# Column loads turned into row loads plus TensorE transposes, and a third buffer for the attention weight groups, in a DMA-bound decode block with its backward pass

## The chip, the cores and the metric

The kernel runs on one core of one Trainium2 chip. The metric is the device time of one execution in microseconds (us), on the slowest core (here the only one). The trace is of one profiled execution, so its span is a little shorter than the timed number: 793.2 us of span belong to a time of about 795 us.

## The reference, cut to what matters

One token goes through an attention block with a cached K and V, and beside it through a SwiGLU MLP. The kernel computes the output and all gradients.

```python
# x: (1,1,640)  k_cache, v_cache: (1,32,8192,128)  wq: (640,4096)  wo: (4096,640)
# w1, w3: (640,1728)  w2: (1728,640); all bf16
xn  = layernorm(x)
q   = xn @ wq                                   # 32 heads of 128
p   = softmax(q . K^T * 128**-0.5)              # per head, 8192 keys
out = x + (p @ V) @ wo + (silu(xn @ w1) * (xn @ w3)) @ w2
# and by jax.vjp, for a given grad_out:
# dx, dk_cache, dv_cache, dwq, dwo, dw1, dw3, dw2
```

K and V of one head are 2 MB each, and so are dK and dV. Over 32 heads 134 MB come in and 134 MB go out; with the weights and their gradients the kernel moves 304.5 MB.

## The kernel before: the parts that matter here

SBUF holds nine 2 MB buffers for K and V tiles (`kv`). dK and dV are written in place into the buffers of K and V and stored from there, so a load of a later head waits for a store of an earlier one. Heads come in 8 groups of 4; each group has its slices of wq and wo (640 KB each), and dwq and dwo are again made in place. Big loads are issued on SyncE's queue (SP), in program order; stores on GpSimd's (POOL); the small loads of x and grad_out on ScalarE's (ACT).

```python
wpool = ctx.enter_context(tc.tile_pool(name="wp", bufs=2))          # L62
tpool = ctx.enter_context(tc.tile_pool(name="tp", bufs=3))          # L63
...
x_bc_bf = consts.tile([P, D], BF16, name="x_bc_bf")                 # L83
nc.scalar.dma_start(x_bc_bf[:], A_x.rearrange("a b d -> (a b d)").partition_broadcast(P))
g_bc = consts.tile([P, D], BF16, name="g_bc")
nc.scalar.dma_start(g_bc[:], grad_out.rearrange("a b d -> (a b d)").partition_broadcast(P))
x_col_bf = consts.tile([P, NC], BF16, name="x_col_bf")
g_col_bf = consts.tile([P, NC], BF16, name="g_col_bf")
with nc.allow_non_contiguous_dma(reason="tiny column-layout loads of x / grad_out"):
    nc.scalar.dma_start(x_col_bf[:], A_x.rearrange("a b (c p) -> p (a b c)", p=P))
    nc.scalar.dma_start(g_col_bf[:], grad_out.rearrange("a b (c p) -> p (a b c)", p=P))
...
def load_group(g):                                                  # L113
    wq_g = wpool.tile([P, NC, GW], BF16, name="wq_g", tag="wq_g")
    nc.sync.dma_start(wq_g[:], wq_v[:, :, g * GW:(g + 1) * GW])
    wo_g = wpool.tile([P, GH, D], BF16, name="wo_g", tag="wo_g")
    nc.sync.dma_start(wo_g[:], wo_v[:, g * GH:(g + 1) * GH, :])
...
nc.vector.tensor_copy(XN_rep[:], xn_col[:].unsqueeze(2).to_broadcast([P, NC, P]))   # L196
nc.vector.tensor_copy(G_rep[:], g_col[:].unsqueeze(2).to_broadcast([P, NC, P]))
...
def prep_group(g):                                                  # L212, start of a group
    for ci in range(NC):
        nc.tensor.matmul(ps_q[:, 0:GW], lhsT=XN_rep[:, ci, :], rhs=wq_g[:, ci, :],
                         start=(ci == 0), stop=(ci == NC - 1))
    ...
bc_sb = consts.tile([P, 2, F], BF16, name="bc_sb")                  # L394, kept to the end
...
for wi in range(2):                                                 # L453, in mlp()
    for b0 in range(0, NB, 4):
        dg = small.tile([P, 4, P // 2, 2], BF16, name="dgm", tag="dg", bufs=1)
        nc.vector.tensor_tensor(dg..., id2..., dgu2[:, wi, ...], ALU.mult)   # diagonal blocks
        nc.tensor.matmul(pb[:, 0:bn * P], lhsT=ones_bf[:], rhs=dg..., start=True, stop=True)
        nc.scalar.copy(bc_sb[:, wi, f0:f1], pb[:, 0:f1 - f0])                # a row on all partitions
...
for h in range(2, H):                                               # L519
    if hh == 1 and g + 1 < NG:
        load_group(g + 1)
    if hh == GH - 1 and g + 1 < NG:
        prep_group(g + 1)
    if h + 1 < H:
        phase_a(h + 1)     # scores, softmax, p @ V
        phase_t(h + 1)     # dP, dS
    phase_b(h)             # dV, dK in place, and their stores
    load_kv(2)
    if hh == GH - 1:
        finish_group(g)    # dwo, dwq in place, and their stores
...                        # dx, then:
mlp_grads()                # dW1 from bc_sb[:,0], dW3 from bc_sb[:,1], then dW2: 6.6 MB
```

The MLP itself runs early, between heads 2 and 3; its weights lie in four of the nine `kv` buffers until then. The gradients of its weights are made at the very end, in tiles oA (most of dW1), oB (most of dW3), oD (most of dW2) and oC (the rests of all three).

## Time and profile before

| What | Value |
|---|---|
| Time, median of 3 runs | 793.3 us (791.96 to 795.97) |
| Moved, mean over the span | 304.5 MB, 384 GB/s |
| Busy: DVE, PE, ACT | 69%, 74%, 40% |
| First projection matmul | 35.16 us |
| First and last dV store issued | 60.77 us and 755.70 us |

No compute engine is full and the DMA engines nearly are, so the question is where they are not. The table by windows gives, for each stretch, its length, the busy time of each engine (with its instructions in brackets), and at the end of each line the granted TensorE clock, the busy share of the DMA engines and the rate in GB/s. Kernel before:

```profile
core 0: us, PE busy (x) PEld busy (x) DVE busy (x) ACT busy (x) POOL busy (x), PEclk, DMA share, GB/s
0.00:51.50 51.50, 15.21 (x205) 11.46 (x205) 10.50 (x24) 13.88 (x17) 1.08 (x8) 1.00 0.97 364
51.50:62.00 10.50, 9.92 (x208) 9.56 (x207) 7.70 (x13) 6.99 (x10) 0.68 (x1) 0.84 0.03 8
62.00:150.00 88.00, 75.20 (x1244) 58.48 (x1242) 66.10 (x108) 32.48 (x49) 2.67 (x5) 0.77 0.89 347
150.00:720.00 570.00, 454.30 (x8407) 391.92 (x8404) 415.51 (x572) 253.32 (x351) 39.72 (x66) 0.78 1.00 410
720.00:750.00 30.00, 24.14 (x448) 20.16 (x447) 24.92 (x33) 8.53 (x14) 1.60 (x3) 0.77 0.51 212
750.00:793.20 43.20, 7.08 (x128) 5.93 (x127) 25.08 (x57) 3.16 (x5) 9.39 (x12) 0.50 0.92 354
235.00:520.00 285.00, 223.48 (x4123) 192.66 (x4121) 207.49 (x290) 120.80 (x170) 19.76 (x33) 0.78 1.00 406
```

Read the last two columns downwards. The middle is full. There are three holes: 51.5 to 62 (8 GB/s), 62 to 150 (347 GB/s) and 720 to 750 (212 GB/s). The reasons stand in the list of waits (engine and line that waited, what released it, then the total in us, how many times, the longest). Kernel before, lines picked out:

```profile
PE pF L217 <- DVE XN_rep L196: 35.2, 1, 35.2
PE pF L217 <- DMA wq_g<-in_A_wq_dram: 30.7, 4, 12.9
PE pT L234 <- DMA wo_g<-in_A_wo_dram: 22.9, 4, 7.6
...
DVE x_col L192 <- DMA x_col_bf<-in_A_x_dram: 16.4, 1, 16.4
DVE g_col L193 <- DMA g_col_bf<-in_grad_out_dram: 8.6, 1, 8.6
```

The same list for SyncE's own DMA queue, kernel before, one line:

```profile
SPq L115 <- DMA out_dram<-wq_g: 70.9, 6, 12.5
```

And the timeline of the kernel before (start, duration, engine, line, what it writes and reads; in square brackets the idle time before it and what ended it), a few lines of DVE, PE and POOL:

```profile
23.35 0.17 DVE L192 CAST x_col<-x_col_bf 128x5 f32<-128x5 bf16 x1 [16.38 <-DMA x_col_bf<-in_A_x_dram]
32.14 0.17 DVE L193 CAST g_col<-g_col_bf 128x5 f32<-128x5 bf16 x1 [8.62 <-DMA g_col_bf<-in_grad_out_dram]
...
653.56 1.04 PE L217 MATMUL pF<-wq_g,XN_rep 128*128 128x512 bf16 x2 [12.90 <-DMA wq_g<-in_A_wq_dram]
...
760.11 0.66 POOL L349 DMA_DIRECT2D out_dram<-Kt  x1 [3.87 <-DVE od_bf L355]
...
766.90 0.86 POOL L488 DMA_DIRECT2D out_dram<-oA  x1
769.19 0.75 POOL L491 DMA_DIRECT2D out_dram<-oB  x1 [1.43 <-DVE oB L490]
773.82 2.09 POOL L494 DMA_DIRECT2D out_dram<-oD  x1 [3.88 <-DVE oD L493]
```

Together they tell this. Two loads of 1.2 KB land at 23 and 32 us; the layernorm and with it all compute begins only then, at 35 us. By 51 us all nine buffers are full and nothing is finished, so nothing can be stored and nothing loaded: the first hole. At group starts TensorE waits for wq_g and wo_g (53.6 us in 8 waits), because their loads wait on the SP queue until the dwq store of two groups earlier has freed one of two buffers. The second hole (62 to 150 us) covers the MLP stage; these lines do not explain it, only that VectorE was busy 66 of its 88 us. The last stall at a group start ends at 653.56 us and leaves compute late for the last heads, where no loads are left to fill the queue: the last hole. In the tail the MLP gradients follow the last dK store closely (oA 6.8 us after it), because `bc_sb` has been ready since the MLP ran.

The queue that carried the x and grad_out loads, kernel before, from the page's table of DMA queues (packets, MB, share of the 16 engines' time):

```profile
q10 hardware_dynamic: 1600, 0.33, 0.3%
```

1600 packets for 0.33 MB: the column layout breaks into one packet of two bytes per element, 1280 of them for the two columns.

### The profile page before, as it was taken

How to read it: one execution, taken by the hardware profiler on the slowest of the kernel's cores; microseconds unless marked ns; L12 is line 12 of the kernel's file. 1: busy time of each engine (PE TensorE's matmuls, PEld its weight loads, DVE VectorE, ACT ScalarE, POOL GpSimd, SP SyncE). 2: the span in 40 equal slices, each digit the busy share in tenths (PEclk: the TensorE clock that was granted, in tenths of full speed). 3: DMA queues.
4: the chain of work that ended last, by engine and by line, in shares of the span. 5: the costliest groups of instructions: out<-in, count | busy, mean ns of one | idle time of the engine just before them, and what ended most of it. 6: DMA issues, size and time to landing. Idle time of an engine off the chain costs nothing. (4 is left out here: it accounts for less than half of the span.)

```text
span 793.2 us, 23350 instructions
## 1 busy us (share of the span) xinstructions
PE 585.9 (74%) x10623; PEld 497.5 (63%) x10623; DVE 549.8 (69%) x804; ACT 318.4 (40%) x444; POOL 55.1 (7%) x95
## 2 busy tenths in 40 slices
PE   0297889889885978699496968698696939699620
PEld 0175668788665966598376857597476827588520
DVE  1158469977758865888189845887289836788890
ACT  0072324554351843275153643285153634276010
POOL 0000000010000100010001000010001000010022
PEclk9996659968776976888587967789587967679555
DMA  8968988899999999999999999999999999996598
GB/s 323 379 247 326 383 339 321 335 411 419 416 430 373 426 417 419 379 409 409 428 406 389 426 416 425 362 422 419 428 410 389 425 421 408 380 420 285 242 390 303
DMA packets 36487, 304.51 MB, mean 384 GB/s; under 512 B 4148, under 2 KB 15348, under 8 KB 20004
## 3 DMA queue, kind: packets, MB, share of 16 engines
q1 hardware_dynamic: 21828, 151.35, 47.9%
q0 software_dynamic: 12960, 151.34, 46.1%
q8 instruction: 83, 1.36, 0.7%
q10 hardware_dynamic: 1600, 0.33, 0.3%
q14 instruction: 16, 0.13, 0.0%
HBM read 151.67 MB, written 151.34 MB: 382 GB/s over the span
## 5 line engine op out<-in xcount | busy, mean ns | idle before, releaser
L262 ACT COPY KT<-pT 128x1024 bf16<-128x1024 bf16 x256 | 242.6, 1038 | 48.5 <-PE pT L260 47.0
L305 PE MATMUL dp<-T,ident_bf 128*128 128x256 bf16 x1024 | 180.7, 312 | 1.7 <-issue 0.8
L260 PE MATMUL pT<-ident_bf,Kt 128*128 128x128 bf16 x2048 | 168.0, 228 | 0.0
L303 DVE TENSOR_TENSOR T<-Vt,do_g 128x2048 bf16<-128x2048 bf16 x128 | 154.3, 1215 | 11.4 <-ACT do_g L243 8.1
L260 PEld LDWEIGHTS <-Kt 128*128 128x128 bf16 x2048 | 131.2, 103 | 3.0 <-issue 0.5
L305 PEld LDWEIGHTS <-ident_bf 128*128 128x128 bf16 x1024 | 103.3, 111 | 25.3 <-issue 3.9
L265 PEld LDWEIGHTS <-KT 128*128 128x128 bf16 x2048 | 78.3, 98 | 35.8 <-ACT KT L262 24.7
L265 PE MATMUL sA<-qc_g,KT 128*128 128x1 bf16 x2048 | 89.0, 165 | 11.7 <-ACT KT L262 4.9
L323 PEld LDWEIGHTS <-Kt 128*128 128x128 bf16 x2048 | 59.3, 101 | 36.1 <-issue 34.8
L325 ACT COPY od_g<-sA 128x2 f32<-128x2 f32 x32 | 5.1, 160 | 164.8 <-PE sA L323 108.0
L287 PEld LDWEIGHTS <-Vt 128*128 128x128 bf16 x2048 | 56.4, 97 | 19.1 <-issue 17.3
L217 PE MATMUL pF<-wq_g,XN_rep 128*128 128x512 bf16 x40 | 18.6, 591 | 65.8 <-DVE XN_rep L196 35.2
L346 POOL DMA_DIRECT2D out_dram<-Vt x32 | 17.6, 549 | 519.4 <-DVE junk L314 244.2
L217 PEld LDWEIGHTS <-XN_rep 128*128 128x128 bf16 x40 | 3.7, 118 | 69.0 <-DVE XN_rep L196 35.2
L236 ACT COPY KT<-pT 128x1024 bf16<-128x1024 bf16 (+1 forms) x24 | 19.8, 874 | 54.7 <-PE pT L234 54.7
L318 DVE COPY negD<-sA 128x1 f32<-128x1 f32 x32 | 5.0, 155 | 47.3 <-PE sA L315 45.6
L271 DVE TENSOR_REDUCE gmax<-sA 1x1 f32<-1x128 f32 x32 | 8.8, 276 | 36.7 <-PE sA L269 36.6
L234 PE MATMUL pT<-ident_bf,wo_g 128*128 128x128 bf16 x160 | 17.2, 283 | 22.9 <-DMA wo_g<-in_A_wo_dram 22.9
L278 ACT ACTIVATE E<-sA,negM 128x64 f32<-128x64 f32 x32 | 10.4, 325 | 56.5 <-DVE negM L275 56.4
L234 PEld LDWEIGHTS <-wo_g 128*128 128x128 bf16 x160 | 14.6, 131 | 23.7 <-DMA wo_g<-in_A_wo_dram 23.5
L349 POOL DMA_DIRECT2D out_dram<-Kt x32 | 17.3, 542 | 151.5 <-DVE negM L275 40.2
L308 DVE TENSOR_REDUCE DP<-dp 128x64 f32<-128x256 f32 x32 | 13.3, 416 | 20.7 <-PE dp L305 20.7
(390 smaller groups left out, 841.1 us busy)
## 6 DMA issues: line engine op xcount, KB each, us to landing
Kt<-in_A_k_cache_dram SPq DMA_DIRECT2D x32, 2048.0 KB, 13.6
Vt<-in_A_v_cache_dram SPq DMA_DIRECT2D x32, 2048.0 KB, 12.0
out_dram<-Vt POOLq DMA_DIRECT2D x32, 2048.0 KB, 12.9
out_dram<-Kt POOLq DMA_DIRECT2D x32, 2048.0 KB, 14.2
wq_g<-in_A_wq_dram SPq DMA_DIRECT2D x8, 640.0 KB, 13.3
wo_g<-in_A_wo_dram SPq DMA_DIRECT2D x8, 640.0 KB, 23.2
out_dram<-wo_g POOLq DMA_DIRECT2D x8, 640.0 KB, 17.9
out_dram<-wq_g POOLq DMA_DIRECT2D x8, 640.0 KB, 18.9
```

Of the source, the lines that this page charges most:

```text
L217: nc.tensor.matmul(ps_q[:, 0:GW], lhsT=XN_rep[:, ci, :], rhs=wq_g[:, ci, :], start=(ci == 0), stop=(ci == NC - 1))
L234: nc.tensor.transpose(pT[:, k, :], wo_g[:, hh, ci * P:(ci + 1) * P], ident_bf[:])
L236: nc.scalar.copy(wT[:, 0:len(bl), :], pT[:, 0:len(bl), :])
L260: nc.tensor.transpose(pT[:, k, :], K3[:, 8 * c + k, :], ident_bf[:])
L262: nc.scalar.copy(KT[:], pT[:])
L265: nc.tensor.matmul(sA[:, j:j + 1], lhsT=KT[:, k, :], rhs=qcol, start=(j == 0), stop=True, skip_group_check=True)
L287: nc.tensor.matmul(sA[:, OC:OC + 1], lhsT=V3[:, j, :], rhs=P2[:, j, 0:1], start=False, stop=(j == J - 1), skip_group_check=True)
L303: nc.vector.tensor_tensor(T3, V3[:, :, ds_], do_h[:, ds_].unsqueeze(1).to_broadcast([P, J, QD]), ALU.mult)
L305: nc.tensor.matmul(dp[:], lhsT=ident_bf[:], rhs=T3[:, :, R * i:R * (i + 1)], start=(q == 0 and i == 0), stop=(q == DH // QD - 1 and i == Q ...
L323: nc.tensor.matmul(sA[:, OC + 1:OC + 2], lhsT=K3[:, j, :], rhs=U2[:, j, 0:1], start=False, stop=(j == J - 1), skip_group_check=True)
L346: nc.gpsimd.dma_start(dvc[h], Vt[:])
L349: nc.gpsimd.dma_start(dkc[h], Kt[:])
```

## The change

It has three parts. (1) x and grad_out come in as five rows of 256 bytes each, TensorE transposes them into columns, and the layernorm sums are made by a matmul with ones. The replicated tiles XN_rep and G_rep go; the matmuls read the column with stride 0 instead. (2) wq_g and wo_g get a third buffer each, so weights can come a group earlier. (3) These cost SBUF, and it is paid for by dropping `bc_sb` (6.9 KB per partition): the broadcast MLP rows are built one at a time in a T buffer (`make_bc`), once in the MLP and a second time for the gradients at the end.

```diff
-    x_bc_bf = consts.tile([P, D], BF16, name="x_bc_bf")
-    nc.scalar.dma_start(x_bc_bf[:], A_x.rearrange("a b d -> (a b d)").partition_broadcast(P))
+    xg_row = consts.tile([NC, 2, P], BF16, name="xg_row")
+    nc.scalar.dma_start(xg_row[:, 0, :], A_x.rearrange("a b (c p) -> (a b c) p", p=P))
+    nc.scalar.dma_start(xg_row[:, 1, :], grad_out.rearrange("a b (c p) -> (a b c) p", p=P))
 ...
-        nc.scalar.dma_start(x_col_bf[:], A_x.rearrange("a b (c p) -> p (a b c)", p=P))
-        nc.scalar.dma_start(g_col_bf[:], grad_out.rearrange("a b (c p) -> p (a b c)", p=P))
 ...
-        wq_g = wpool.tile([P, NC, GW], BF16, name="wq_g", tag="wq_g")
+        wq_g = wpool.tile([P, NC, GW], BF16, name="wq_g", tag="wq_g", bufs=3)
-        wo_g = wpool.tile([P, GH, D], BF16, name="wo_g", tag="wo_g")
+        wo_g = wpool.tile([P, GH, D], BF16, name="wo_g", tag="wo_g", bufs=3)
 ...
+    for i in range(2):
+        nc.tensor.transpose(ps_x[:, i, 0:NC], xg_row[:, i, :], ident_bf[0:NC, 0:NC])
+    nc.vector.tensor_copy(xg_col[:], ps_x[:, :, 0:NC])
 ...   # sums by matmul with ones_f instead of a reduction over x_bc_bf
-            nc.tensor.matmul(ps_q[:, 0:GW], lhsT=XN_rep[:, ci, :], rhs=wq_g[:, ci, :],
+            nc.tensor.matmul(ps_q[:, 0:GW], lhsT=xn_col_bf[:, ci:ci + 1].to_broadcast([P, P]), rhs=wq_g[:, ci, :],
 ...   # and the same for G_rep
-    bc_sb = consts.tile([P, 2, F], BF16, name="bc_sb")
+    def make_bc(wi):
+        bc = t_tile()
+        ...   # the loop over b0 from mlp(), still with one dg buffer, into bc
+        return bc
 ...
         for wi in range(2):                       # in mlp()
+            bc = make_bc(wi)
 ...
+        for wi in range(2):                       # in mlp_grads()
+            bc = make_bc(wi)
+            da, db, dv = ((d1a, d1b, dw1_v), (d3a, d3b, dw3_v))[wi]
+            ...   # dW1 or dW3 from bc, and their stores; dW2 follows as before
```

More of the change, by code (lines that the diff above doesn't have):

```diff
@@ L81 @@
     dw3_v = out_7.rearrange("(ci p) f -> p ci f", p=P)
-    x_bc_bf = consts.tile([P, D], BF16, name="x_bc_bf")
-    nc.scalar.dma_start(x_bc_bf[:], A_x.rearrange("a b d -> (a b d)").partition_broadcast(P))
+    xg_row = consts.tile([NC, 2, P], BF16, name="xg_row")
+    nc.scalar.dma_start(xg_row[:, 0, :], A_x.rearrange("a b (c p) -> (a b c) p", p=P))
+    nc.scalar.dma_start(xg_row[:, 1, :], grad_out.rearrange("a b (c p) -> (a b c) p", p=P))
     g_bc = consts.tile([P, D], BF16, name="g_bc")
     nc.scalar.dma_start(g_bc[:], grad_out.rearrange("a b d -> (a b d)").partition_broadcast(P))
-    x_col_bf = consts.tile([P, NC], BF16, name="x_col_bf")
-    g_col_bf = consts.tile([P, NC], BF16, name="g_col_bf")
-    with nc.allow_non_contiguous_dma(reason="tiny column-layout loads of x / grad_out"):
-        nc.scalar.dma_start(x_col_bf[:], A_x.rearrange("a b (c p) -> p (a b c)", p=P))
-        nc.scalar.dma_start(g_col_bf[:], grad_out.rearrange("a b (c p) -> p (a b c)", p=P))
     NB = (F + P - 1) // P
@@ L168 @@
     DXN0 = OUT0 + NC
-    negmean = consts.tile([P, 1], F32, name="negmean")
-    rstd = consts.tile([P, 1], F32, name="rstd")
-    x_col = consts.tile([P, NC], F32, name="x_col")
-    g_col = consts.tile([P, NC], F32, name="g_col")
-    xn_col = consts.tile([P, NC], F32, name="xn_col")
-    xn_col_bf = consts.tile([P, NC], BF16, name="xn_col_bf")
-    XN_rep = consts.tile([P, NC, P], BF16, name="XN_rep")
-    G_rep = consts.tile([P, NC, P], BF16, name="G_rep")
-    msum = small.tile([P, 1], F32, name="msum")
-    nc.vector.tensor_reduce(msum[:], x_bc_bf[:], AX.X, ALU.add)
-    nc.vector.tensor_scalar(negmean[:], msum[:], -1.0 / D, None, ALU.mult)
-    xc_t = tpool.tile([P, 1024], F32, name="xc", tag="T")
-    xc = xc_t[:, 0:D]
-    nc.vector.tensor_scalar(xc, x_bc_bf[:], negmean[:], None, ALU.add)
-    xsq_t = tpool.tile([P, 1024], F32, name="xsq", tag="T")
-    xsq = xsq_t[:, 0:D]
-    sumsq = small.tile([P, 1], F32, name="sumsq")
-    nc.vector.scalar_tensor_tensor(xsq, xc, 1.0, xc, ALU.mult, ALU.mult, accum_out=sumsq[:])
-    std = small.tile([P, 1], F32, name="std")
-    nc.scalar.activation(std[:], sumsq[:], ACTF.Sqrt, bias=eps_t[:], scale=1.0 / D)
-    nc.vector.reciprocal(rstd[:], std[:])
-    nc.vector.tensor_copy(x_col[:], x_col_bf[:])
-    nc.vector.tensor_copy(g_col[:], g_col_bf[:])
-    nc.vector.tensor_scalar(xn_col[:], x_col[:], negmean[:], rstd[:], ALU.add, ALU.mult)
-    nc.vector.tensor_copy(xn_col_bf[:], xn_col[:])
-    nc.vector.tensor_copy(XN_rep[:], xn_col[:].unsqueeze(2).to_broadcast([P, NC, P]))
-    nc.vector.tensor_copy(G_rep[:], g_col[:].unsqueeze(2).to_broadcast([P, NC, P]))
     def t_tile():
@@ L209, in pst_f @@
         return ps_t.tile([P, 512], F32, name="pF", tag="pT")
+    negmean = consts.tile([P, 1], F32, name="negmean")
+    rstd = consts.tile([P, 1], F32, name="rstd")
+    xg_col = consts.tile([P, 2, NC], F32, name="xg_col")
+    x_col = xg_col[:, 0, :]
+    g_col = xg_col[:, 1, :]
+    g_col_bf = consts.tile([P, NC], BF16, name="g_col_bf")
+    xn_col = consts.tile([P, NC], F32, name="xn_col")
+    xn_col_bf = consts.tile([P, NC], BF16, name="xn_col_bf")
+    ps_x = ps_t.tile([P, 2, 8], BF16, name="ps_x", tag="pT")
+    for i in range(2):
+        nc.tensor.transpose(ps_x[:, i, 0:NC], xg_row[:, i, :], ident_bf[0:NC, 0:NC])
+    nc.vector.tensor_copy(xg_col[:], ps_x[:, :, 0:NC])
+    nc.vector.tensor_copy(g_col_bf[:], g_col)
+    msum = small.tile([P, 1], F32, name="msum")
+    nc.vector.tensor_reduce(msum[:], x_col, AX.X, ALU.add)
+    ps_m = pst_f()
+    nc.tensor.matmul(ps_m[:, 0:1], lhsT=ones_f[:], rhs=msum[:], start=True, stop=True)
+    nc.vector.tensor_scalar(negmean[:], ps_m[:, 0:1], -1.0 / D, None, ALU.mult)
+    xc = small.tile([P, NC], F32, name="xc", bufs=1)
+    nc.vector.tensor_scalar(xc[:], x_col, negmean[:], None, ALU.add)
+    xsq = small.tile([P, NC], F32, name="xsq", bufs=1)
+    sumsq = small.tile([P, 1], F32, name="sumsq")
+    nc.vector.scalar_tensor_tensor(xsq[:], xc[:], 1.0, xc[:], ALU.mult, ALU.mult, accum_out=sumsq[:])
+    ps_v = pst_f()
+    nc.tensor.matmul(ps_v[:, 0:1], lhsT=ones_f[:], rhs=sumsq[:], start=True, stop=True)
+    std = small.tile([P, 1], F32, name="std")
+    nc.scalar.activation(std[:], ps_v[:, 0:1], ACTF.Sqrt, bias=eps_t[:], scale=1.0 / D)
+    nc.vector.reciprocal(rstd[:], std[:])
+    nc.vector.tensor_scalar(xn_col[:], x_col, negmean[:], rstd[:], ALU.add, ALU.mult)
+    nc.vector.tensor_copy(xn_col_bf[:], xn_col[:])
     def prep_group(g):
@@ L238, in prep_group @@
                 ci = bl[k0][0]
-                nc.tensor.matmul(ps_do[:, 0:GW], lhsT=G_rep[:, ci, :],
+                nc.tensor.matmul(ps_do[:, 0:GW], lhsT=g_col_bf[:, ci:ci + 1].to_broadcast([P, P]),
                                  rhs=wT[:, k0:k0 + GH, :].rearrange("p h d -> p (h d)"),
@@ L393 @@
     blocks_f = [(b, min(P, F - b * P)) for b in range(NB)]
-    bc_sb = consts.tile([P, 2, F], BF16, name="bc_sb")
+    dgu2 = consts.tile([P, 2, NB, 2], BF16, name="dgu2")
+    def make_bc(wi):
+        bc = t_tile()
+        id2 = ident_bf[:].rearrange("p (a b) -> p a b", b=2)
+        for b0 in range(0, NB, 4):
+            bn = min(4, NB - b0)
+            dg = small.tile([P, 4, P // 2, 2], BF16, name="dgm", tag="dg", bufs=1)
+            nc.vector.tensor_tensor(dg[:, 0:bn], id2.unsqueeze(1).to_broadcast([P, bn, P // 2, 2]),
+                                    dgu2[:, wi, b0:b0 + bn, :].unsqueeze(2).to_broadcast([P, bn, P // 2, 2]),
+                                    ALU.mult)
+            pb = pst_f()
+            nc.tensor.matmul(pb[:, 0:bn * P], lhsT=ones_bf[:],
+                             rhs=dg[:, 0:bn].rearrange("p k a b -> p (k a b)"), start=True, stop=True)
+            f0 = b0 * P
+            f1 = min(F, f0 + bn * P)
+            nc.scalar.copy(bc[:, f0:f1], pb[:, 0:f1 - f0])
+        return bc
     hcol = consts.tile([P, NB], F32, name="hcol")
@@ L449, in mlp @@
         nc.vector.tensor_tensor(dgu[:, 0, :], dgu[:, 0, :], t1[:], ALU.mult)
-        dgu2 = consts.tile([P, 2, NB, 2], BF16, name="dgu2")
         nc.vector.tensor_copy(dgu2[:], dgu[:].unsqueeze(3).to_broadcast([P, 2, NB, 2]))
-        id2 = ident_bf[:].rearrange("p (a b) -> p a b", b=2)
-        for wi in range(2):
-            for b0 in range(0, NB, 4):
-                bn = min(4, NB - b0)
-                dg = small.tile([P, 4, P // 2, 2], BF16, name="dgm", tag="dg", bufs=1)
-                nc.vector.tensor_tensor(dg[:, 0:bn], id2.unsqueeze(1).to_broadcast([P, bn, P // 2, 2]),
-                                        dgu2[:, wi, b0:b0 + bn, :].unsqueeze(2).to_broadcast([P, bn, P // 2, 2]),
-                                        ALU.mult)
-                pb = pst_f()
-                nc.tensor.matmul(pb[:, 0:bn * P], lhsT=ones_bf[:],
-                                 rhs=dg[:, 0:bn].rearrange("p k a b -> p (k a b)"), start=True, stop=True)
-                f0 = b0 * P
-                f1 = min(F, f0 + bn * P)
-                nc.scalar.copy(bc_sb[:, wi, f0:f1], pb[:, 0:f1 - f0])
         FC = 384
         for wi in range(2):
+            bc = make_bc(wi)
             wa, wb = ((w1a, w1b), (w3a, w3b))[wi]
@@ L473, in mlp @@
                 nc.vector.tensor_tensor(T3[:, 0:NA, :], wa[:, :, f0:f0 + fn],
-                                        bc_sb[:, wi, f0:f0 + fn].unsqueeze(1).to_broadcast([P, NA, fn]), ALU.mult)
-                nc.vector.tensor_tensor(T3[:, NA, :], wb[:, f0:f0 + fn], bc_sb[:, wi, f0:f0 + fn], ALU.mult)
+                                        bc[:, f0:f0 + fn].unsqueeze(1).to_broadcast([P, NA, fn]), ALU.mult)
+                nc.vector.tensor_tensor(T3[:, NA, :], wb[:, f0:f0 + fn], bc[:, f0:f0 + fn], ALU.mult)
                 for i in range(fn // RX):
@@ L485, in mlp_grads @@
         d1a, d3a, d1b, d3b, d2a, d2b = split_views(oA, oB, oC, oD)
-        for ci in range(NA):
-            nc.vector.tensor_scalar(d1a[:, ci, :], bc_sb[:, 0, :], xn_col[:, ci:ci + 1], None, ALU.mult)
-        nc.gpsimd.dma_start(dw1_v[:, 0:NA, :], d1a)
-        for ci in range(NA):
-            nc.vector.tensor_scalar(d3a[:, ci, :], bc_sb[:, 1, :], xn_col[:, ci:ci + 1], None, ALU.mult)
-        nc.gpsimd.dma_start(dw3_v[:, 0:NA, :], d3a)
+        for wi in range(2):
+            bc = make_bc(wi)
+            da, db, dv = ((d1a, d1b, dw1_v), (d3a, d3b, dw3_v))[wi]
+            for ci in range(NA):
+                nc.vector.tensor_scalar(da[:, ci, :], bc[:, 0:F], xn_col[:, ci:ci + 1], None, ALU.mult)
+            nc.gpsimd.dma_start(dv[:, 0:NA, :], da)
+            nc.vector.tensor_scalar(db, bc[:, 0:F], xn_col[:, NA:NC], None, ALU.mult)
+            nc.gpsimd.dma_start(dv[:, NA, :], db)
         for b in range(NBA):
@@ L494, in mlp_grads @@
         nc.gpsimd.dma_start(out_8[0:NBA * P, :].rearrange("(fb p) c -> p fb c", p=P), d2a)
-        nc.vector.tensor_scalar(d1b, bc_sb[:, 0, :], xn_col[:, NA:NC], None, ALU.mult)
-        nc.gpsimd.dma_start(dw1_v[:, NA, :], d1b)
-        nc.vector.tensor_scalar(d3b, bc_sb[:, 1, :], xn_col[:, NA:NC], None, ALU.mult)
-        nc.gpsimd.dma_start(dw3_v[:, NA, :], d3b)
         for b in range(NBA, NB):
@@ L539 @@
     nc.vector.tensor_tensor(dxn[:], acc_sb[:, NC:2 * NC], dxm[:], ALU.add)
-    nc.vector.tensor_tensor(fin[:, 0:NC], acc_sb[:, 0:NC], x_col[:], ALU.add)
+    nc.vector.tensor_tensor(fin[:, 0:NC], acc_sb[:, 0:NC], x_col, ALU.add)
     st = consts.tile([P, 2], F32, name="st")
@@ L551 @@
     nc.vector.tensor_scalar(t5[:], t5[:], nst[:, 0:1], rstd[:], ALU.add, ALU.mult)
-    nc.vector.tensor_tensor(fin[:, NC:2 * NC], t5[:], g_col[:], ALU.add)
+    nc.vector.tensor_tensor(fin[:, NC:2 * NC], t5[:], g_col, ALU.add)
     ps_o = pst_f()
```

## The prediction

> **What bounds the kernel now.** The table by windows gives the DMA engines' busy share: 1.00 from 150 to 720 us (410 GB/s), where only bytes count. Three holes are not DMA-bound: 51.5-62 us (share 0.03, about 10 us lost), 62-150 us (0.89, 10 us) and 720-750 us (0.51, 15 us). The queue table's shares sum to 95%: about 754 of 793 us are DMA work, 40 us gaps.
>
> Hole 1: in the timeline TensorE starts at 35.2 us. The waits blame x_col_bf (16.4 us, landed 23.3) and g_col_bf (8.6 more, landed 32.1). All nine K/V buffers are full by 51 us, but the first store is issued at 60.8, 25.6 us after compute began. The Trainium skill ("DMA: Bandwidth & Descriptors", Rules for kernel authors) says a strided last dimension lowers to one descriptor per element; the trace agrees: two 1.2 KB loads needed 21 and 30 us, and their queue moved 1600 packets for 0.33 MB.
>
> Hole 3: at group starts TensorE waits for wq_g (30.7 us in 4 waits, longest 12.9) and wo_g (22.9 us in 4), because the load waits on the SP queue for the dwq store of two groups earlier (70.9 us, 6 waits). The last stall, 640.5-653.6 us, leaves compute late for the last heads; the DMA runs dry at 720-750.
>
> **What the change does.**
> 1. Column loads become row loads of five 256-byte runs, then some 12 small dependent steps, estimated at 4-5 us from steps of 0.15-0.35 us in the trace. XN_rep and G_rep (0.8 us each) go. Compute should start near 9-11 us, limited by wq_g too (landing 7-9 us): 25 us earlier. The DMA can use only the gaps of 51-150 us: 16-20 us gained.
> 2. Third wq_g/wo_g buffer: weights arrive one group ahead, so TensorE's wait for them vanishes. The instruction order shows the SP queue still waiting for a dwq store in nearly the same place, now for a later group, so the 70.9 us should largely stay, harmlessly. In the DMA-bound middle nothing is gained; before the last heads compute is up to 13 us less late, filling part of hole 3: 6-12 us gained.
> 3. Cost: two more rounds of make_bc: 8 dgm multiplies (0.28-0.42 us), 8 matmuls (0.28-0.63), 8 ScalarE copies (0.32-0.59), serial through one dg buffer, estimated 5 us per round. They stand after the last head, behind the final dx chain. The oA store was issued 6.8 us after the last dK store; I estimate 15-17 us now, and oD (2 MB) last, about 27 us after. Part hides under queued stores: 2-6 us lost. In the MLP stage bc takes one of three T buffers: mostly hidden.
>
> **Sum.** 793 - 18 - 9 + 4 (tail), less 2 us for the vanished small packets: **768 us**, range **757 to 781**. Faster by over 2%: 0.84; within 2%: 0.15; slower: 0.01.
>
> **What would show it.** Right: first projection matmul near 10 us; first dV store near 36; no DMA hole at 51-62; no TensorE wait for wq_g after the first group; DMA share of the 30 us before the last dV store well above 0.5; a new DMA gap of several us before oA; the middle at share 1.00 and about 410 GB/s. Wrong: first matmul later than 15 us, or holes again at 90-150 us (VectorE-bound MLP stage).
>
> **What would make it wrong.** The middle may run at a lower rate. Compute (about 18 us per head against 20 us of DMA) may not stay ahead, since TensorE's granted clock falls to 0.5 after pauses; then hole 3 stays: near 778. If both gains are complete and the tail hides, 757.

## The result, and the profile after

The changed kernel took 767.26 us (median of 4 runs, 766.19 to 768.71), the kernel before in the same rounds 794.63 us (4 runs, 791.96 to 796.4). The ratio is 0.9659, 95% interval 0.9623 to 0.9696. Ratios here are the mean time of one kernel's fast runs over that of the other's of the same rounds, so they are not quite the ratios of the medians quoted.

The table by windows of the kernel after, with the columns as above:

```profile
0.00:51.50 51.50, 37.72 (x584) 29.66 (x584) 29.74 (x50) 22.34 (x30) 2.29 (x10) 0.90 0.97 381
51.50:62.00 10.50, 6.71 (x79) 3.81 (x80) 9.55 (x14) 0.16 (x1) 1.07 (x2) 0.58 1.03 431
62.00:150.00 88.00, 73.08 (x1255) 60.35 (x1254) 57.44 (x108) 34.78 (x51) 2.90 (x5) 0.77 0.93 374
105.00:135.00 30.00, 28.32 (x537) 24.56 (x534) 25.50 (x34) 16.65 (x24) 1.60 (x3) 0.94 0.79 311
150.00:690.00 540.00, 453.06 (x8225) 387.55 (x8224) 403.57 (x549) 250.01 (x345) 37.88 (x63) 0.78 1.00 415
690.00:720.00 30.00, 21.94 (x428) 18.39 (x426) 25.85 (x31) 8.53 (x14) 2.14 (x4) 0.70 0.76 316
720.00:764.50 44.50, 9.44 (x72) 4.96 (x71) 24.75 (x62) 7.16 (x12) 7.74 (x11) 0.50 0.79 307
235.00:520.00 285.00, 236.96 (x4345) 203.94 (x4342) 213.63 (x290) 135.09 (x184) 19.93 (x33) 0.79 1.01 423
```

The first hole is gone (431 GB/s against 8). The late one, now in 690 to 720, is shallower (316 against 212). The tail got worse (307 over the last 44.5 us against 354 over the last 43.2). And two lines were not foreseen: 105 to 135 is still a hole (the prediction had named holes in 90 to 150 as a sign of being wrong), and in the full middle, at nearly the same share (1.00 and 1.01), the rate went up from 406 to 423 GB/s between 235 and 520.

Waits of the kernel after, the line that is left of TensorE's waits for weights (there is none for wq_g):

```profile
PE pT L233 <- DMA wo_g<-in_A_wo_dram: 7.4, 1, 7.4
```

The SP queue's own waits, kernel after, one line:

```profile
SPq L111 <- DMA out_dram<-wq_g: 52.4, 4, 13.6
```

So the queue still waits for dwq stores, as expected, but for a buffer that is needed a group later.

The timeline of the kernel after, lines of PE, DVE and POOL that answer to those of before:

```profile
2.13 0.18 PE L189 MATMUL ps_x<-ident_bf,xg_row 5*128 5x5 bf16 x1 [2.13 <-DMA xg_row<-in_A_x_dram]
5.72 0.18 PE L189 MATMUL ps_x<-ident_bf,xg_row 5*128 5x5 bf16 x1 [3.41 <-DMA xg_row<-in_grad_out_dram]
...
9.41 2.32 PE L216 MATMUL pF<-wq_g,xn_col_bf 128*128 128x512 bf16 x5 [1.08 <-DVE xn_col_bf L208]
...
83.55 0.42 DVE L401 TENSOR_TENSOR dgm<-ident_bf,dgu_161 128x512 bf16<-128x512 bf16 x1 [0.82 <-PE pF L405]
...
726.24 0.65 POOL L348 DMA_DIRECT2D out_dram<-Kt  x1 [3.87 <-DVE od_bf L354]
...
742.12 0.78 POOL L494 DMA_DIRECT2D out_dram<-oA  x1 [9.07 <-DVE oA L493]
...
748.41 0.88 POOL L494 DMA_DIRECT2D out_dram<-oB  x1 [4.95 <-DVE oB L493]
...
752.67 1.03 POOL L499 DMA_DIRECT2D out_dram<-oD  x1 [2.83 <-DVE oD L498]
```

Compute starts at 9.41 us instead of 35.16. In the tail oA leaves 15.9 us after the last dK store instead of 6.8, and the 2 MB of oD 26.4 us after it instead of 13.7. From the last dK store to the end it is 38.3 us instead of 33.1: the tail costs 5.2 us more. The queue of the small loads went down to 164 packets:

```profile
q10 hardware_dynamic: 164, 0.17, 0.1%
```

To see where the 28.7 us between the two profiled spans come from, I added up the GB/s of 5-us windows and noted when each kernel had moved a given number of megabytes. The kernels move the same bytes to 0.2 MB, so the lead at equal bytes tells where time was won or lost. Each curve is one execution, and not always a typical one (the profiled runs of e_rows, e_bufs2 and w2first2 were the slowest of their kernels, those of e_colsync and e_dg2 the fastest), and the two profiled runs of the changed kernel, after and after2, differ by up to 3 us, so a difference of 2 or 3 us between two curves is not evidence. In us, each kernel's lead over the profiled run of the kernel before (the labels of the other kernels are those of the experiments below):

```
MB moved     20    40    50   120   200   280   290   303
after      12.4  20.1  21.4  20.5  29.3  26.0  33.7  27.5
e_rows     12.3  20.2  23.9  20.5  18.5  16.9  19.0  19.0
e_bufs2    12.3  20.2  19.3  17.3  16.8  14.7  15.0   8.6
e_colsync  10.2  18.2  23.7  23.3  25.5  25.4  26.3  26.1
w2first2   12.2  20.0  20.9  19.3  27.1  26.4  29.9  28.8
e_dg2      12.4  20.1  25.3  28.1  35.5  34.3  42.6  42.0
```

The start gave 20 us by the time 40 MB had moved. The lead then grew by some 6 us in the middle (20.5 at 120 MB, 26.0 at 280 MB), by 7.7 us at the late hole (280 to 290 MB), and shrank by 6.2 us in the tail (290 to 303 MB).

### The profile page after: what moved, and what is told of

It is laid out like the page before. It is cut to its first block, busy times and chain, and to the rows that moved or that the text cites. A ratio compares the mean times of both kernels' runs of the same rounds, so it can differ in the third digit from the quotient of the medians.

```text
span 764.5 us, 23388 instructions
## 1 busy us (share of the span) xinstructions
PE 601.9 (79%) x10637; PEld 504.7 (66%) x10637; DVE 550.9 (72%) x810; ACT 323.0 (42%) x452; POOL 54.0 (7%) x95
## 5 line engine op out<-in xcount | busy, mean ns | idle before, releaser
L304 PE MATMUL dp<-T,ident_bf 128*128 128x256 bf16 x1024 | 190.5, 324 | 15.1 <-DVE T L302 15.0
L304 PEld LDWEIGHTS <-ident_bf 128*128 128x128 bf16 x1024 | 107.5, 115 | 41.5 <-issue 16.7
L286 PEld LDWEIGHTS <-Vt 128*128 128x128 bf16 x2048 | 57.3, 98 | 19.3 <-issue 17.3
L235 ACT COPY KT<-pT 128x1024 bf16<-128x1024 bf16 (+1 forms) x24 | 19.8, 874 | 40.9 <-PE pT L233 40.9
L378 ACT COPY KT<-pT 128x1024 bf16<-128x1024 bf16 (+1 forms) x24 | 19.3, 877 | 2.3 <-PE pT L376 2.2
L274 DVE COPY negM<-sA 128x1 f32<-128x1 f32 x32 | 4.9, 152 | 21.1 <-PE sA L271 21.0
L314 PE MATMUL sA<-rdot,negones_f 128*128 128x1 f32 x64 | 13.6, 282 | 7.8 <-DVE junk L313 7.8
## 6 DMA issues: line engine op xcount, KB each, us to landing
Vt<-in_A_v_cache_dram SPq DMA_DIRECT2D x32, 2048.0 KB, 23.4
out_dram<-wq_g POOLq DMA_DIRECT2D x8, 640.0 KB, 25.3
```

What stands on the lines that cost most here:

```text
L235: nc.scalar.copy(wT[:, 0:len(bl), :], pT[:, 0:len(bl), :])
L286: nc.tensor.matmul(sA[:, OC:OC + 1], lhsT=V3[:, j, :], rhs=P2[:, j, 0:1], start=False, stop=(j == J - 1), skip_group_check=True)
L304: nc.tensor.matmul(dp[:], lhsT=ident_bf[:], rhs=T3[:, :, R * i:R * (i + 1)], start=(q == 0 and i == 0), stop=(q == DH // QD - 1 and i == Q ...
L378: nc.scalar.copy(wT[:, 0:len(bl), :], pT[:, 0:len(bl), :])
```

## The experiments

My theory was that of the prediction: the early start and the third buffer are two separate gains in two separate holes, and the rebuilt rows cost a little at the end. The rivals were that the start alone does it all (compute being ahead, weights would come in time too); that the strided loads cost by their packets rather than by their lateness; and that the third buffer gains where the DMA engines are full already. All ten runs gave correct results. The kernel before had a median of 796.03 us beside the first four, 794.86 beside the next three and 796.93 beside the last three.

### e_rows: the start alone

The kernel before with the row loads, the transposes and the stride-0 weights of the change. Two buffers and `bc_sb` stay.

```diff
-    nc.scalar.dma_start(x_bc_bf[:], A_x.rearrange("a b d -> (a b d)").partition_broadcast(P))
-        nc.scalar.dma_start(x_col_bf[:], A_x.rearrange("a b (c p) -> p (a b c)", p=P))
-        nc.scalar.dma_start(g_col_bf[:], grad_out.rearrange("a b (c p) -> p (a b c)", p=P))
+    nc.scalar.dma_start(xg_row[:, 0, :], A_x.rearrange("a b (c p) -> (a b c) p", p=P))
+    nc.scalar.dma_start(xg_row[:, 1, :], grad_out.rearrange("a b (c p) -> (a b c) p", p=P))
 ...   # and the layernorm chain and lhsT of the change
```

> The kernel before with the row loads, the layernorm chain on TensorE and the broadcast weights; two weight buffers and the kept broadcast rows, as before. Theory (three separate effects: about 20 us from the earlier start, about 14 us from the third buffer, half of it in the middle and half before the last heads, 6 us lost in the tail): 773 to 776 us, the hole of 15 us before the last heads is still there (DMA share near 0.5 for some 30 us), TensorE waits for wq_g about 30 us in all, and the lead over before, read by bytes moved, stays at 20 us from 50 MB to 280 MB. Rival A (the start is the whole gain, the third buffer worth nothing): about 761 us. Rival B (the start only moves the wait to a later place and the buffer is the gain): 785 us or more.

Measured: 773.13 us, ratio 0.9697 [0.966, 0.9735], 22.9 us less than before. TensorE still waits for wq_g (34.9 us in 3 waits) and wo_g (22.7 in 4), and 700 to 730 us still is a hole (share 0.57, 238 GB/s). Starting earlier did not bring the weights earlier: the first rival falls. One part of the expectation was missed: the lead by bytes did not stay at 20 us, it fell from 23.9 at 50 MB to 16.9 at 280 MB.

### e_bufs2: the changed kernel with two buffers

```diff
-        wq_g = wpool.tile([P, NC, GW], BF16, name="wq_g", tag="wq_g", bufs=3)
+        wq_g = wpool.tile([P, NC, GW], BF16, name="wq_g", tag="wq_g")
-        wo_g = wpool.tile([P, GH, D], BF16, name="wo_g", tag="wo_g", bufs=3)
+        wo_g = wpool.tile([P, GH, D], BF16, name="wo_g", tag="wo_g")
```

> The changed kernel with the weight groups back at two buffers, the rebuilding kept. Theory: the start gain of 20 us stays, the 14 us of the third buffer go; part of the tail cost of 6 us stays: 777 to 782 us. Rival A (the buffer is worth nothing): 767 us, as the changed kernel. TensorE's wait for wq_g comes back at about 30 us, and the lead by bytes does not grow between 120 and 160 MB, if that growth of 6 us belongs to the buffer; if it grows all the same, it belongs to something else.

Measured: 780.7 us, ratio 0.9785 [0.9745, 0.9825], within what was expected; TensorE's wait for wq_g came back at 41.9 us in 4 waits, more than the 30 expected. Two readings follow. Against e_rows, which differs only in `bc_sb`, rebuilding the rows costs 7.6 us. Against the changed kernel the third buffers are worth 13 us by medians; by ratios 10 (0.9785 against 0.9659) to 12 (against the changed kernel's 0.9635 in its later run). The profiled run of this kernel was its slowest (785.55), so its curve above is some 5 us low at the end.

The middle of this kernel, from its table by windows:

```profile
235.00:520.00 285.00, 226.90 (x4248) 197.91 (x4246) 210.44 (x287) 134.32 (x185) 20.70 (x34) 0.80 1.00 409
```

With two buffers the stretch that ran at 423 GB/s runs at 409, at nearly the same DMA share. e_rows has 407 there, the kernel before 406, and e_colsync below, also with two buffers, 411. With three buffers but the old start, e_cols below has 418. So the higher rate comes with the third buffers and with nothing else in the change.

A mean over 285 us hides what happens inside. At one group start of e_bufs2 TensorE waited 16.3 us for wq_g, no store was issued for 33 us, and the DMA then ran dry. In the timeline of e_bufs2, PE and POOL:

```profile
369.02 1.03 PE L216 MATMUL pF<-wq_g,xn_col_bf 128*128 128x512 bf16 x2 [16.30 <-DMA wq_g<-in_A_wq_dram]
...
386.68 0.53 POOL L345 DMA_DIRECT2D out_dram<-Vt  x1 [33.04 <-DVE junk L313]
```

And in the tables by windows, first of e_bufs2, then of e_rows:

```profile
385.00:390.00 5.00, 4.81 (x115) 4.21 (x112) 5.00 (x6) 3.79 (x6) 0.53 (x1) 1.00 0.69 288
```

```profile
380.00:385.00 5.00, 4.51 (x49) 3.45 (x48) 3.50 (x5) 1.84 (x3) 0.00 (x0) 0.87 0.64 272
385.00:390.00 5.00, 4.83 (x123) 4.40 (x120) 5.00 (x6) 3.79 (x5) 0.53 (x1) 1.00 0.56 236
```

In windows of 5 us the kernel after never falls below a share of 0.97 between 235 and 520 us, and TensorE waits for no weights there. So part of what the third buffers gave in the middle was the filling of ordinary holes.

### e_cols: the changed kernel with column loads

```diff
-    nc.scalar.dma_start(xg_row[:, 0, :], A_x.rearrange("a b (c p) -> (a b c) p", p=P))
-    nc.scalar.dma_start(xg_row[:, 1, :], grad_out.rearrange("a b (c p) -> (a b c) p", p=P))
+        nc.scalar.dma_start(xg_cb[:, 0, :], A_x.rearrange("a b (c p) -> p (a b c)", p=P))
+        nc.scalar.dma_start(xg_cb[:, 1, :], grad_out.rearrange("a b (c p) -> p (a b c)", p=P))
 ...   # the two transposes go, the sums on TensorE stay
```

> The changed kernel with the two column loads of 2-byte elements put back on the ACT queue in place of the row loads and transposes; all else kept (three buffers, rebuilding, layernorm sums on TensorE). Theory: first projection matmul at 33 to 36 us, DMA idle again for about 10 us near 52 to 62 us and 8 to 10 us more before 150 us: 785 to 789 us. Rival B (the start is not worth its 20 us): 767 to 772 us.

Measured: 788.11 us, ratio 0.9884 [0.9842, 0.9926]. The first hole is back, in the table by windows of this kernel:

```profile
51.50:62.00 10.50, 10.11 (x259) 9.94 (x257) 8.14 (x11) 7.77 (x9) 0.68 (x1) 0.83 0.19 78
```

VectorE waits 27.0 us for the columns. Taking the start away costs 21 us by medians against the changed kernel's 767.26 (18 by the ratios), about what adding it gave. The layernorm sums on TensorE bring little by themselves while the data are late: the first projection matmul runs at 32.5 us.

### e_colsync: the kernel before, with the same column loads on the queue of the big loads

Two words differ from the kernel before. The strided loads stay; they go to the SP queue, where they stand ahead of the weights, instead of to ACT's queue beside them.

```diff
-        nc.scalar.dma_start(x_col_bf[:], A_x.rearrange("a b (c p) -> p (a b c)", p=P))
-        nc.scalar.dma_start(g_col_bf[:], grad_out.rearrange("a b (c p) -> p (a b c)", p=P))
+        nc.sync.dma_start(x_col_bf[:], A_x.rearrange("a b (c p) -> p (a b c)", p=P))
+        nc.sync.dma_start(g_col_bf[:], grad_out.rearrange("a b (c p) -> p (a b c)", p=P))
```

> The kernel before with its two 2-byte-element column loads issued on the SP queue ahead of the weights, instead of on the ACT queue beside them; nothing else. Theory (each element's tiny packet waits its turn behind bulk packets of another queue): ahead of the bulk in the same queue they land within 12 us, the first projection matmul comes by 15 us, and the time falls by 14 to 20 us with no TensorE transposes at all: 774 to 781 us. Rival (the elements themselves cost 21 and 9 us wherever they are issued): first projection matmul at 30 us or later and 790 us or more, as the bulk loads now queue behind them.

Measured: 770.23 us, ratio 0.9699 [0.9676, 0.9722], better than I had expected and as good as e_rows (0.9697). The timeline of this kernel, DVE:

```profile
6.02 0.17 DVE L192 CAST x_col<-x_col_bf 128x5 f32<-128x5 bf16 x1 [0.65 <-DMA x_col_bf<-in_A_x_dram]
8.04 0.17 DVE L193 CAST g_col<-g_col_bf 128x5 f32<-128x5 bf16 x1 [1.85 <-DMA g_col_bf<-in_grad_out_dram]
```

The same two loads land at 6.0 and 8.0 us instead of 23.4 and 32.1, and the first projection matmul runs at 12.22. The page counts 36488 packets, 4149 of them under 512 bytes, one more than before. So neither the layout nor the number of packets made the loads late by itself; it took megabytes of another queue moving beside them. (The run changes the queue and the place in time together: the first load is issued at 0.74 us instead of 1.68. Column loads issued first on ACT's own queue were not run. The changed kernel's row loads stay on that second queue, beside the same megabytes, and with a few packets each are in use at 2.13 and 5.72 us: it is many packets and a shared turn together that cost.)

This agrees with the Trainium skill, "DMA: Bandwidth & Descriptors", section "Queues, rings and completion order": each DMA engine takes turns between the queue rows that have work, a packet at a time. The trace shows these turns. It records each DMA packet with its start and size; counted from these records, the 18 us from 10 to 28 us of the kernel before hold 496 packets of two bytes on ACT's queue and 464 packets of 16 KB on SP's, one for one, so the column loads moved at the pace of the K and V loads. In e_cols, where the same loads stood beside weight packets of 1.0 to 1.3 KB at first, 868 of the 1280 two-byte packets were through by 8 us; the others, beside 16-KB packets, took until 27.6 us. In e_colsync all had gone by 7.6 us.

### e_wq3: one third buffer instead of two

e_rows with the third buffer for wq_g alone, which fits beside `bc_sb` when five small tiles of the softmax and layernorm get one buffer instead of two. Both third buffers beside `bc_sb` do not fit even so (a build is refused, 0.3 KB per partition short), so "the third buffers without the rebuilding" was not run. The single buffers are a second difference from e_rows, and what they cost was not measured.

```diff
-        wq_g = wpool.tile([P, NC, GW], BF16, name="wq_g", tag="wq_g")
+        wq_g = wpool.tile([P, NC, GW], BF16, name="wq_g", tag="wq_g", bufs=3)
-        E = small.tile([P, J], F32, name="E")
+        E = small.tile([P, J], F32, name="E", bufs=1)
 ...   # and bufs=1 for junk, msum, sumsq, std
```

> Row loads, a third buffer for wq_g alone, two for wo_g, and the broadcast rows kept (no rebuilding; two scratch tiles and three one-use tiles single-buffered to fit). Theory (the group start needs both weights, so wo_g becomes the wait): TensorE's waits for wq_g go, those for wo_g stay at 15 us or more in all, and the gain over the row loads alone (773.1) is only part: 765 to 771 us. Rival (the wq_g wait is the whole of it): 759 to 763 us, the changed kernel less its rebuilding.

Measured: 768.8 us, ratio 0.9673 [0.9625, 0.972], within the interval of e_rows. Its waits:

```profile
PE pT L233 <- DMA wo_g<-in_A_wo_dram: 59.2, 6, 14.7
```

The wait for wq_g is gone, and the one for wo_g grew from 22.7 to 59.2 us; on the SP queue loads now wait for dwo stores (25.8 us) and dwq stores (22.5 us). The stall moved to the other tile. One buffer of the two, with these single buffers, is worth 2 us by ratios and 4 by medians, little beside the 10 to 13 us of both.

### e_w2first: dW2 first in the tail

The changed kernel with the loop that makes dW2, which needs no broadcast row, moved ahead of the two `make_bc` rounds.

```diff
     def mlp_grads():
+        for b in range(NBA):            # dW2 (oD) and its stores, unchanged
+            ...
         for wi in range(2):
             bc = make_bc(wi)
             ...
-        for b in range(NBA):
-            ...
```

> The changed kernel with the dW2 products and their stores, which need no broadcast rows, moved ahead of the rebuilt rows in the tail. Theory (the tail costs 6 us because no store is ready for the DMA while the rows are rebuilt): the dW2 store is issued within 6 us of the last dwq store, the DMA gap before the oA store shrinks by about 5 us: 760 to 764 us. Rival (the 6 us are the added work itself, serial at the end whatever the order): 766 to 768 us.

Measured: 761.36 us, ratio 0.9565 [0.9524, 0.9606]. oD is issued 1.8 us after the dwq store, and its 2 MB move while the rows are rebuilt. The window in which the changed kernel's DMA ran dry, in the table by windows first of the kernel after, then of e_w2first:

```profile
740.00:750.00 10.00, 1.77 (x4) 0.31 (x3) 8.35 (x20) 2.08 (x4) 2.76 (x4) 0.50 0.59 231
```

```profile
740.00:750.00 10.00, 2.21 (x4) 0.42 (x4) 7.12 (x14) 2.13 (x5) 2.26 (x4) 0.50 0.96 356
```

By medians that is 5.9 us under the changed kernel's 767.26, and 5.0 in the later run beside it on one chip: the tail's cost (5.2 us) is won back by an order. It was not a cost of work: VectorE was busy 7.1 of these 10 us, against 8.4 in the kernel after. It was 2 MB of stores, which need nothing of the chain, standing behind it.

### e_spread: the MLP gradients among the last heads

e_w2first with the three parts of `mlp_grads` moved forward, behind heads 29, 30 and 31, to fill the late hole.

```diff
         load_kv(2)
+        if h == H - 3:
+            mlp_grads_w2()
+        if h >= H - 2:
+            mlp_grads_w13(h - (H - 2))
...
-    mlp_grads()
```

> The changed kernel with the MLP gradients moved forward among the last heads: dW2 after the third-last head, dW1 after the second-last, dW3 after the last. Theory (the remaining gaps, about 10 us before the last dV store and about 10 us after the last dwq store, are the DMA without a ready store, while the added VectorE work is the same wherever it stands): both gaps mostly close: 748 to 755 us. Rival (VectorE bounds the last heads, and work put before them delays the stores by as much as it fills): 760 to 767 us.

Measured: 759.98 us, ratio 0.9578 [0.9547, 0.9608]: no better than e_w2first, so this expectation was missed, and the rival (760 to 767 us) held. The DMA share of 690 to 720 us rose only from 0.70 to 0.82. VectorE, which makes these gradients, had been busy 25.9 of those 30 us in e_w2first already, and is busy 26.0 here; the dV stores of the last heads came later (head 30 at 715.4 us against 712.3) and the last dwq store at 745.2 us. What seemed idle time for the DMA was not idle time for the engine that would have had to fill it.

### e_dg2, e_w2first2 and after2: two dg buffers in the rebuilding

e_dg2 is e_w2first with two buffers for the diagonal blocks, so that VectorE can make the next block while TensorE reads this one. The edit also doubles the block that shares this tag in `finish_group`; the two are not separated. It ran beside repeats of e_w2first and of the changed kernel, five rounds on one chip.

```diff
-        dg = small.tile([P, GH, P], BF16, name="dg", bufs=1)
+        dg = small.tile([P, GH, P], BF16, name="dg", bufs=2)
-            dg = small.tile([P, 4, P // 2, 2], BF16, name="dgm", tag="dg", bufs=1)
+            dg = small.tile([P, 4, P // 2, 2], BF16, name="dgm", tag="dg", bufs=2)
```

> The changed kernel with dW2 first in the tail and with two dg scratch buffers instead of one. Theory (the rebuilding rounds run serially because VectorE waits about 0.67 us per round for TensorE to free the one dg buffer): oA is issued about 2 us and oB about 3 us earlier, 2 to 3 us less than the same kernel with one dg buffer run beside it. Rival (the tail is by now filled by the DMA, or bound by ScalarE's copies): no difference beyond 1 us.

> The changed kernel with dW2 first in the tail, one dg buffer, a repeat of an earlier run, so that it and the two-buffer version run on one chip: 760 to 763 us.

> The changed kernel itself again, on the chip of these runs, for direct ratios: 766 to 769 us, 5 to 7 us above dW2-first.

Measured: e_dg2 756.16 us (751.9 to 761.46), ratio 0.9503 [0.9457, 0.9549]; e_w2first2 761.88, 0.9573 [0.9539, 0.9608]; after2 766.83, 0.9635 [0.9598, 0.9673]. e_dg2 beats both kernels, by 5% and by about 11 us. The two repeats came as expected. e_dg2 gained 5.7 us over its neighbour where I expected 2 to 3. In the tail the stores of oA and oB stand 4.0 us apart (733.60 and 737.63) instead of 6.3 (746.82 and 753.11): 2.3 us, as expected. By the curves the rest arose in the MLP stage. The table by windows there, of e_dg2 and of e_w2first2:

```profile
100.00:135.00 35.00, 30.43 (x541) 26.26 (x543) 30.05 (x38) 16.96 (x25) 1.60 (x3) 0.95 0.94 383
```

```profile
100.00:135.00 35.00, 33.48 (x597) 29.04 (x599) 30.57 (x39) 19.05 (x26) 1.12 (x3) 0.95 0.82 328
```

By 50 MB e_dg2 leads the kernel before by 25.3 us and e_w2first2 by 20.9; by 120 MB by 28.1 and 19.3. But the profiled execution of e_dg2 was its fastest and that of e_w2first2 its slowest (12.7 us apart, the medians 5.7), so the curves overstate what the second buffer gave. VectorE did wait for the single block in the MLP stage too (0.82 us in the line at 83.55 us of the kernel after). That this wait makes the hole at 105 to 135 us is not shown: e_rows and e_colsync have the same single block and rebuild nothing, and the one has the hole (0.78, 313 GB/s), the other only a trace of it (0.93, 372 GB/s). The six times of e_dg2 spread over 10 us, three at 752 to 753.5 and three at 759 to 761.5; those of the kernel before beside it spread as far (790.0 to 799.63), its two neighbours over 4 to 5; why stays open. Its interval overlaps that of e_w2first2 slightly, so the size of the gain is uncertain.

## Why the prediction was right, point by point

The predicted time was 768, the measured 767. The start, the buffers and the tail each did what was said, but each term of the sum was too small, and the errors cancelled. One chain of kernels gives the terms: before, e_rows, e_bufs2, after.

| Term | Predicted | By medians | By ratios, of 796 us |
|---|---|---|---|
| Start (before to e_rows) | -18 (-16 to -20), and -2 for small packets | -22.9 | -24 |
| Rebuilding rows (e_rows to e_bufs2) | +4 (+2 to +6), in the tail | +7.6 | +7 |
| Third buffers (e_bufs2 to after) | -9 (-6 to -12) | -13.4 | -10 to -12 |

- **Bound and holes: right.** The first hole went with the late columns (e_cols brings it back), and the late one shrank with the third buffers (e_rows and e_bufs2, both with two, keep a share of 0.57 and 0.59 in 700 to 730 us).
- **Start: right in mechanism and time of start** (9.41 us against "near 10", first dV store at 34.60 us against "near 36"), a little too small in size. By 40 MB the lead is 20.1 us; e_rows gives 22.9 in the end.
- **"less 2 us for the vanished small packets": not supported.** e_colsync keeps every small packet and gains as much as e_rows. The Trainium skill, "DMA: Bandwidth & Descriptors", section "Rules for kernel authors", on which the prediction leaned, is right about the lowering (1308 packets under 512 bytes vanish with the change), but the packets as such were not what cost: 0.3% of the engines' time on their queue.
- **Third buffer: right in mechanism** (no wait for wq_g, 7.4 us left for wo_g, the SP queue's wait 52.4 us and harmless), **too small in size.** The wrong step is "In the DMA-bound middle nothing is gained". About half of what the buffers gave came there: from 120 to 280 MB the lead of the changed kernel grew by 5.5 us, while those of e_rows and e_bufs2 fell by 3.6 and 2.6 (that of e_colsync, also with two buffers, grew by 2.1). The premise was that a mean DMA share of 1.00 means that only bytes count. It failed in two ways, by the packet records of 235 to 520 us. First, the mean hid holes: unrounded, the share is 0.992 in e_rows and 0.995 in e_bufs2, with the dry windows shown under e_bufs2, against 1.009 in the kernel after. Second, busy is not equally fast: a 16-KB packet takes 611 ns in the median in all four kernels, but those of the K and V loads take 651 ns in the mean before, 639 and 635 in e_rows and e_bufs2, and 615 after. For e_rows and e_bufs2 each of the two makes up about half of the lower rate; the kernel before has no such hole in this stretch, and there it is mostly the second. Why some load packets take longer with two buffers is not shown.
- **Tail: right** (oA 15.9 us after the last dK store against "15-17", oD 26.4 against "about 27", cost 5.2 us of "2-6"). The curves of e_rows and e_bufs2 agree: from 290 to 303 MB the first stays level, the second loses 6.4 us. e_w2first shows that it was a matter of order.
- **"In the MLP stage bc takes one of three T buffers: mostly hidden": neither shown nor refuted.** At 50 MB e_rows leads the kernel after by 2.5 us and e_bufs2 by 4.6; at 120 MB e_rows and after stand level at 20.5. The sign "holes again at 90-150" came true in part: 311 GB/s from 105 to 135 us. It was named as a sign of a wrong prediction, but e_rows, which rebuilds nothing, has the same hole (313 GB/s), so it does not come from bc. VectorE was busy 25.5 of these 30 us; what makes the hole stays open.

## What to carry to other kernels

When compute waits for a tiny load, look first at the queue that it shares engines with: issuing it ahead of the bulk on the same queue gave the whole gain of the new start, for two words. A buffer that removes a stall pays also where the DMA share says full; cut such a stretch into windows of 5 us and compare GB/s before calling it untouchable. When a rebuilt value sits in front of stores, let the stores that don't need it go first (5 to 6 us here), and try two small buffers for the rebuilding (another 5.7 us by medians, less certain).

## What the Trainium skill lacked or had wrong

- "DMA: Bandwidth & Descriptors", "Rules for kernel authors": for a strided last dimension it advises to rearrange. It lacks that for a tiny load the order of issue can matter as much: the same strided 1.2 KB loads were used at 6.0 and 8.0 us at the head of the big loads' queue, and at 23.4 and 32.1 us on a second queue, behind two loads of 160 KB.
- The same page, "Queues, rings and completion order": it tells that engines take turns by packets, but gives no figure for what a small load loses by it beside bulk traffic. Here it was 17 us for the first and 24 us for the second load, with one two-byte packet moved per 16-KB packet (496 to 464 from 10 to 28 us).
- The same page, "Specifications" and "Where 436 GB/s comes from": it says that about 358 GB/s of the HBM side bind a core's transfers between HBM and SBUF. This run, with one core in use, held 423 GB/s for 285 us. The page's own table under "Measured" fits better (425 GB/s for 16 MB, a single core with the pair's other core idle), and so does "Perfetto Trace Analysis", "Engine Utilization", in its part "Roofline": a core alone can go to about 435 GB/s.
- "Perfetto Trace Analysis", "Identifying the Most-Contended Engine", calls the occupancy of the DMA engines misleading, and the runs agree: at a share that rounds to 1.00 or 1.01, 285 us ran at 406, 409 or 423 GB/s.
- No page that I looked at says what matmul weights read with stride 0 cost. Here nothing that shows: the weight loads had a median of 104 ns from XN_rep and 104 ns from the broadcast column, and 96 and 97 ns for the second pair.
